# Rewriting the skipped general path as loops, and moving the bound check, the flag load and the low-part products in an attention-and-gated-MLP kernel

## The chip, the cores and the metric

The kernel runs on one core of a Trainium2 chip. The metric is the device time of one execution in microseconds (us). A core has a tensor engine (PE, whose weight loads are listed as PEld), a vector engine (DVE), a scalar engine (ACT), GpSimd (POOL) and SyncE (SP), each with its own queue of instructions that it works through in order; they wait for each other by semaphores. Here SP issues nearly all DMAs, and ACT issues output DMAs too.

## The reference

First a recurrent linear attention over 768 positions for 4 batches and 8 heads of 48, then a gated MLP on the result.

```python
for t in range(S):                       # S = 768, state is D x D per head, D = 48
    cur = einsum('bhd,bhe->bhde', u * k_t, v_t)
    y[:, :, t] = einsum('bhd,bhde->bhe', r_t, state + cur)
    state = w_t[..., None] * state + einsum('bhd,bhe->bhde', k_t, v_t)
x = y as (3072 tokens, 384)
out = (sigmoid(x @ w_gate) * (x @ w_val)) @ w_out      # 384 -> 1536 -> 384
```

## The kernel before

The 768 positions are cut into 6 blocks of 128; a block with its 4 batches is 512 tokens, and the attention of one batch in one block is a unit `q` of 24. The MLP runs over the 6 blocks `n` and, inside each, over 12 pieces `f` of the hidden width. All its products are made from a high and a low part of each operand: `whi` and `wlo` of the weights, `x` in two parts, and of the hidden values `hh` (high) and `hl` (low); each product is three (low x high, high x low, high x high).

One step (n, f) of the MLP in the later blocks: `gate` makes nine products into the bank `pg`, `sigmoid` (ACT) reads it into `sg`; `value` makes nine products into `pu`; `hidden` (DVE) multiplies into `sg`; `hidden_hi` (ACT, line 516) casts to `hh`; `hidden_lo` (DVE, line 520) subtracts to `hl`; `down_turned` makes nine products into the three banks `po` (line 546). A step's down products are issued one step later, after the value products of the next step; the variable `last` holds them back. At f = 11 `down_turned` also copies the three banks out (ACT for k = 0 and 2, line 554; in the last block DVE for k = 1, line 552) and issues the output DMAs (line 556).

Blocks 0 and 1 and the first attention units are ordered by a planner (`Plan`), which the change does not touch. From block 2 on the order is the loop at the end of `tile_kernel`: `n` over blocks 2 to 5, `j` over four batches, `i` over three pieces, so f = 3j + i. Between the MLP's parts stand those of the attention for block n + 1; in block 5 there are none left.

The fast path holds only while certain sums stay within bounds. After step (5, 0) `check_bounds` compares four tables of sums (lines 559 to 562, into `fine`), DVE adds them up into `count` (line 564), one product with a column of `ones` adds over the partitions into `total` (line 566), and DVE writes the word `flag` (line 567). At the very end every engine loads `flag` into a register (line 694) and branches: if it is not 0, `general` computes everything again in another way. With the inputs of the reference the flag is 0, and every engine jumps over `general`. Line 723 is the end of the program, where SP waits for the others and all engines meet in a barrier.

In the built program the weights of all 12 pieces, `flag`, `ones` and the states lie one behind the other in a pool of constants; `count` lies in another pool.

Of the kernel before, what the change touches and what calls it, by code (L numbers as in the profile page):

```python
# [9 lines left out]
F32 = mybir.dt.float32  # L10
# [11 lines left out]
P = 128  # L22
# [19 lines left out]


@with_exitstack
def general(ctx: ExitStack, tc: tile.TileContext, dec, tok, wts, u, out, whi, wlo, ident):


    nc = tc.nc
    pool = ctx.enter_context(tc.tile_pool(name="general", bufs=1))
    bank = ctx.enter_context(tc.tile_pool(name="banks", bufs=1, space=PSUM))  # L50
    rows = ctx.enter_context(tc.tile_pool(name="rows", bufs=1, space=bass.MemoryType.DRAM)).tile([NC_, B, C, DM], F32, name="rows")

    def tiles(name, shape, dtype=F32):
        return pool.tile(shape, dtype, name=name)

    raw, t, full, square = tiles("raw", [P, HW], mybir.dt.int64), tiles("t", [P, HW], I32), tiles("full", [P, HW]), tiles("square", [P, HW])
    for f in range(NFF):
        for half in range(2):
            cols = slice(half * HW, (half + 1) * HW)
            nc.sync.dma_start(raw, wts[f][:, cols])  # L60
# [12 lines left out]
            nc.vector.tensor_tensor(out=full, in0=full, in1=part, op=ALU.add)  # L73
            nc.scalar.copy(whi[f][:, cols], full)
            nc.vector.tensor_tensor(out=wlo[f][:, cols], in0=full, in1=whi[f][:, cols].bitcast(F32), op=ALU.subtract)
# [12 lines left out]
    ub = ul.unsqueeze(1).unsqueeze(3).broadcast_to(shape)  # L88
    py = [bank.tile([P, 512], F32, name=f"py{i}") for i in range(2)]
    values = tok.rearrange("(b c) t (n p o e) -> c n o t b p e", b=B, n=3, o=2, e=D)  # L90
    for c in range(NC_):
        for b in range(B):
            nc.sync.dma_start(d[:, b], dec[b * NC_ + c])
        with tc.For_i(0, C) as i:
            def at(first, step):
                return d[:, :, first:first + NP * step].rearrange("a b (p c) -> a b p c", c=step)[:, :, :, bass.ds(i, 1)].broadcast_to(shape)
            for o in range(2):
                for b in range(B):
                    nc.sync.dma_start(vb[64 * o:64 * o + D, b], values[c, 2, o, bass.ds(i, 1), b].partition_broadcast(D))
            nc.vector.tensor_tensor(out=kv, in0=vb, in1=at(WW, C), op=ALU.mult)  # L100
            nc.vector.tensor_tensor(out=mix, in0=kv, in1=ub, op=ALU.mult)
            nc.vector.tensor_tensor(out=mix, in0=mix, in1=state, op=ALU.add)
            nc.vector.tensor_tensor(out=mix, in0=mix, in1=at(WW + NP * C, C), op=ALU.mult)
            nc.vector.tensor_tensor(out=state, in0=state, in1=at(1, W1), op=ALU.mult)
            nc.vector.tensor_tensor(out=state, in0=state, in1=kv, op=ALU.add)
            for j in range(2):
                nc.tensor.matmul(py[j][:2, :DM], lhsT=heads, rhs=mix[:, 2 * j:2 * j + 2], start=True, stop=True)
                nc.scalar.copy(y[:, 2 * j:2 * j + 2], py[j][:2, :DM].rearrange("a (b p e) -> a b p e", b=2, e=D))
            for b in range(B):
                for o in range(2):  # L110
                    nc.sync.dma_start(
                        rows[c, b, bass.ds(i, 1)].rearrange("t (p o e) -> o t p e", o=2, e=D)[o], y[o:o + 1, b])
# [5 lines left out]
    def feed(n, b, turned):  # L118
        nc.sync.dma_start(x, rows[n, b])
        for k in range(NKT):  # L120
            nc.tensor.transpose(out=px[:, k * C:(k + 1) * C], in_=x[:, k * P:(k + 1) * P], identity=ident)
        px3 = px[:, :DM].rearrange("a (k c) -> a k c", c=C)
        nc.scalar.copy(xhi, px3)
        nc.vector.tensor_tensor(out=xlo, in0=px3, in1=xhi.bitcast(F32), op=ALU.subtract)
        for f in range(NFF):
            for s, acc in enumerate((pg, pu)):
                for k in range(NKT):
                    cols = slice(s * DM + k * P, s * DM + (k + 1) * P)
                    for j, (w, a) in enumerate(((wlo, xhi), (whi, xlo), (whi, xhi))):
                        nc.tensor.matmul(acc[:, :C], lhsT=w[f][:, cols], rhs=a[:, k], start=k == 0 and j == 0, stop=k == NKT - 1 and j == 2)  # L130
            nc.scalar.activation(gate, pg[:, :C], AF.Sigmoid)
            nc.vector.tensor_tensor(out=h, in0=pu[:, :C], in1=gate, op=ALU.mult)
            nc.scalar.copy(hh, h)
            nc.vector.tensor_tensor(out=hl, in0=h, in1=hh.bitcast(F32), op=ALU.subtract)
            for k in range(NKT if turned else 1):
                cols = slice(2 * DM + k * P, 2 * DM + (k + 1) * P)
                for j, (a, w) in enumerate(((hl, whi), (hh, wlo), (hh, whi))):
                    first, done = f == 0 and j == 0 and k == 0, f == NFF - 1 and j == 2
                    if turned:
                        nc.tensor.matmul(po[:, k * C:(k + 1) * C], lhsT=w[f][:, cols], rhs=a, start=first, stop=done, skip_group_check=True)  # L140
                    else:
                        nc.tensor.matmul(po[:, :DM], lhsT=a, rhs=w[f][:, 2 * DM:], start=first, stop=done)
        nc.scalar.copy(x, po[:, :DM])
        if turned:
            to = out[n].rearrange("(k p b c) -> b p k c", p=P, b=B, c=C)[b]
            nc.sync.dma_start(to, x.rearrange("p (k c) -> p k c", c=C))
        else:
            nc.sync.dma_start(out[n].rearrange("(b c e) -> b c e", b=B, c=C)[b], x)

    for n in range(NC_):  # L150
        for b in range(B):
            feed(n, b, n >= 2)


class Plan:
# [49 lines left out]
def tile_kernel(ctx: ExitStack, tc: tile.TileContext, dec: bass.AP, tok: bass.AP, wts: bass.AP, u: bass.AP, out: bass.AP):  # L205
# [41 lines left out]
    nc.gpsimd.memset(fine, 1.0)  # L247
    flag = const.tile([1, 1], I32, name="flag")
    ones = const.tile([P, 1], F32, name="ones")
    nc.gpsimd.memset(ones, 1.0)  # L250
    state = [const.tile([L, NP, D], F32, name=f"state{b}") for b in range(B)]

# [285 lines left out]
    def down_turned(n, f, i0, i1):  # L538

        hh, hl = hid["hi", n, f, i0], hid["lo", n, f, i0]  # L540
        for k in range(NKT):
            if f == 0:
                po[n, k] = ps1.tile([P, 512], F32, tag=f"po{k}", name=f"po{n}_{k}")
            cols = slice(2 * DM + k * P, 2 * DM + (k + 1) * P)
            for j, (h, w) in enumerate(((hl, whi), (hh, wlo), (hh, whi))):
                nc.tensor.matmul(po[n, k], lhsT=w[f][:, cols], rhs=h, start=f == 0 and j == 0, stop=f == NFF - 1 and j == 2)  # L546
            if f == NFF - 1:
                o = p1.tile([P, B * C], F32, tag=f"ot{k}", name=f"o{n}_{k}")
# [9 lines left out]
    def check_bounds():  # L558
# [1 line left out]
        nc.vector.tensor_scalar(out=fine[:, 1], in0=acc_x, scalar1=0.0, scalar2=0.0, op0=ALU.mult, op1=ALU.is_equal)  # L560
        nc.vector.tensor_scalar(out=fine[:, 2, :NFF], in0=acc_s, scalar1=1e10, scalar2=None, op0=ALU.is_le)
        nc.vector.tensor_scalar(out=fine[:, 3, :NFF], in0=acc_t, scalar1=0.0, scalar2=None, op0=ALU.is_equal)
        count = p1.tile([P, 1], F32, name="count")
        nc.vector.tensor_reduce(out=count, in_=fine, op=ALU.add, axis=AX.XY)
        total = att_bank("total")
        nc.tensor.matmul(total[:1, :1], lhsT=ones, rhs=count, start=True, stop=True)
        nc.vector.tensor_scalar(out=flag, in0=total[:1, :1], scalar1=float(P * 4 * NG), scalar2=None, op0=ALU.not_equal)
# [104 lines left out]
    for n in range(2, NC_):  # L672
        for j in range(B):
            trio = steps((n + 1) * B + j) if n + 1 < NC_ else nothing
            for i in range(3):
# [13 lines left out]
                last.append(a)  # L689
                if n == NC_ - 1 and j == 0 and i == 0:  # L690
                    check_bounds()
    down_turned(*last.pop())
    own.close()
    with tc.If(nc.values_load(flag[:1, :1]) != 0):
        general(tc, dec, tok, wts, u, out, whi, wlo, ident)


# [31 lines left out]
```

## Time and profile before

| | us |
|---|---|
| median of 3 runs | 598.0 |
| the 3 runs | 598.21, 598.0, 595.76 |
| span of the profiled execution, first to last instruction | 593.7 |
| the profiled execution's own time | not given beyond its span |
| PE busy in the span | 555.1 (93%) |
| DVE busy | 332.6 (56%) |
| ACT busy | 200.2 (34%) |
| POOL busy | 96.4 (16%) |

The span is the time from the first to the last instruction of the core; the time of a run contains what lies around it too. Busy time counts computing instructions; loads of registers, branches and waits are not in it, but are listed by source line with their durations. In rows of groups, "x9" is the number of instructions, the first number of a timeline row is the start, the second the time to the end of the last of them. PEclk, the clock granted to PE, is 9 to 10 tenths in all slices but a few at the start, where it is 7 or 8; the mean is 0.989.

### The profile page before, as it was taken

How to read it: one execution, taken by the hardware profiler on the slowest of the kernel's cores; microseconds unless marked ns; L12 is line 12 of the kernel's file. 1: busy time of each engine (PE TensorE's matmuls, PEld its weight loads, DVE VectorE, ACT ScalarE, POOL GpSimd, SP SyncE). 2: the span in 40 equal slices, each digit the busy share in tenths (PEclk: the TensorE clock that was granted, in tenths of full speed). 3: DMA queues.
4: the chain of work that ended last, by engine and by line, in shares of the span. 5: the costliest groups of instructions: out<-in, count | busy, mean ns of one | idle time of the engine just before them, and what ended most of it. 6: DMA issues, size and time to landing. Idle time of an engine off the chain costs nothing.

```text
span 593.7 us, 14287 instructions
## 1 busy us (share of the span) xinstructions
PE 555.1 (93%) x6330; PEld 478.6 (81%) x6330; DVE 332.6 (56%) x571; ACT 200.2 (34%) x397; POOL 96.4 (16%) x86
## 2 busy tenths in 40 slices
PE   4477799999999999999999999999999999999995
PEld 3366699999999999888888888888888888788884
DVE  4989889989675762254644644644544554212121
ACT  2648783434333322322212322212322212222221
POOL 3342011102220503002202202202202200000000
PEclk9998799999999999999999999999999999999999
DMA  8887930022243221122032042032032000100001
GB/s 238 269 332 285 363 94 2 1 88 71 73 135 97 82 70 60 54 87 73 18 88 78 17 135 87 3 87 83 24 124 86 3 1 2 40 15 0 1 0 60
DMA packets 11479, 50.84 MB, mean 86 GB/s; under 512 B 1312, under 2 KB 2464, under 8 KB 9872
## 3 DMA queue, kind: packets, MB, share of 16 engines
q1 hardware_dynamic: 8672, 45.38, 23.7%
q10 hardware_dynamic: 2736, 4.46, 2.0%
q8 instruction: 52, 0.85, 0.6%
q14 instruction: 19, 0.16, 0.1%
HBM read 45.11 MB, written 4.72 MB: 84 GB/s over the span
## 4 chain that ended last, share of the span: by engine, by line
PE 86%; DVE 7%; DMA 3%; issue 1%; ACT 1%; SPq 0%; ACTq 0%; DVEq 0%
PE pu L494 25%; PE pg L494 25%; PE po L546 16%; PE po L529 8%; PE pa L461 3%; PE pa L390 2%; PE pa L400 2%; DMA wraw<-wts 2%; PE pk L373 1%; PE px L473 1%; PE pv L437 1%; DVE eg L341 1%; DMA pin<-dec 1%; PE pa L437 1%; DVE full L275 1%
## 5 line engine op out<-in xcount | busy, mean ns | idle before, releaser
L494 PE MATMUL pu<-x,w 128*128 128x256 f32 (+1 forms) x864 | 171.4, 343 | 0.0
L494 PE MATMUL pg<-x,w 128*128 128x256 f32 (+1 forms) x864 | 169.0, 341 | 1.2 <-DVE w L287 1.2
L494 PEld LDWEIGHTS pg<-x,w 128*128 128x128 f32 x864 | 137.9, 192 | 19.4 <-DVE w L287 1.6
L494 PEld LDWEIGHTS pu<-x,w 128*128 128x128 f32 x864 | 136.7, 192 | 17.1
L512 DVE TENSOR_TENSOR sg<-pu,sg 128x256 f32<-128x256 f32 (+1 forms) x96 | 53.4, 556 | 145.0 <-PE pu L494 144.0
L516 ACT CAST hh<-sg 128x256 fp32r<-128x256 f32 (+1 forms) x96 | 49.1, 512 | 171.2 <-DVE sg L512 170.8
L505 ACT ACTIVATE sg<-pg 128x256 f32<-128x256 f32 (+1 forms) x96 | 46.9, 489 | 139.0 <-PE pg L494 137.7
L546 PE MATMUL po<-hh,w 128*128 128x512 f32 x288 | 89.1, 390 | 0.0
L334 POOL TENSOR_TENSOR bon<-tok,a 128x384 f32<-128x384 f32 x24 | 34.9, 1456 | 277.3 <-DVE a L330 277.3
L520 DVE TENSOR_TENSOR hl<-sg,hh 128x256 fp32r<-128x256 f32 (+1 forms) x96 | 55.2, 575 | 39.1 <-ACT hh L516 39.0
L546 PEld LDWEIGHTS po<-hh,w 128*128 128x128 f32 x288 | 54.1, 188 | 10.8
L546 PE MATMUL po<-hl,w 128*128 128x512 f32 x144 | 58.7, 407 | 0.2 <-DVE hl L520 0.2
L323 POOL TENSOR_TENSOR bon<-tok,ub 128x384 f32<-128x384 f32 x24 | 32.3, 1345 | 114.1 <-DMA tok<-tok 38.4
L529 PE MATMUL po<-w,hh 128*128 128x384 f32 x192 | 49.7, 340 | 0.0
L468 DVE TENSOR_TENSOR bon<-pa,bon 128x192 f32<-128x192 f32 x48 | 15.6, 352 | 48.0 <-PE pa L461 47.9
L529 PE MATMUL po<-w,hl 128*128 128x384 f32 x96 | 34.5, 359 | 6.0 <-DVE hl L520 6.0
L368 ACT ACTIVATE junk<-eg 112x1032 bf16<-112x1032 f32 x24 | 25.6, 1066 | 29.7 <-DVE eg L358 29.6
L529 PEld LDWEIGHTS po<-w,hh 128*128 128x128 f32 x192 | 35.5, 192 | 0.0
L341 DVE TENSOR_TENSOR_SCAN eg<-pin,ends 112x516 f32<-112x516 f32 x24 | 30.0, 1249 | 5.0 <-DMA pin<-dec 5.0
L546 PEld LDWEIGHTS po<-hl,w 128*128 128x128 f32 x144 | 27.0, 188 | 6.2 <-DVE hl L520 0.6
L358 DVE TENSOR_TENSOR_SCAN eg<-pin,heads 112x516 f32<-112x516 f32 x24 | 29.7, 1237 | 0.0
L326 POOL TENSOR_TENSOR bon<-bon,tok 128x384 f32<-128x384 f32 x24 | 27.4, 1140 | 1.7
(68 smaller groups left out, 502.4 us busy)
## 6 DMA issues: line engine op xcount, KB each, us to landing
pin<-dec SPq DMA_DIRECT2D x23, 675.5 KB, 5.3
tok<-tok SPq DMA_DIRECT2D x24, 576.0 KB, 5.8
wraw<-wts SPq DMA_DIRECT2D x12, 1152.0 KB, 12.3
y<-o ACTq DMA_DIRECT2D x11, 256.0 KB, 2.1
y<-o ACTq DMA_DIRECT2D x8, 192.0 KB, 1.9
pin<-dec SPq DMA_DIRECT2D x1, 448.0 KB, 4.0
y<-o SPq DMA_DIRECT2D x1, 256.0 KB, 2.9
pin<-dec SPq DMA_DIRECT2D x1, 227.5 KB, 2.8
```

The costliest lines, as they stand in the source:

```text
L323: nc.gpsimd.tensor_tensor(out=bon[q], in0=tk[q][:, 0:DM], in1=ub, op=ALU.mult)
L326: nc.gpsimd.tensor_tensor(out=bon[q], in0=bon[q], in1=tk[q][:, DM:2 * DM], op=ALU.mult)
L334: nc.gpsimd.tensor_tensor(out=by_head(bon[q]), in0=by_head(tk[q][:, 2 * DM:]), in1=a0, op=ALU.mult)
L341: nc.vector.tensor_tensor_scan(out=e[:, 516:0:-1], data0=t[:, 516:0:-1], data1=ends[:, 516:0:-1], initial=0.0, op0=ALU.mult, op1=ALU.add,)
L358: nc.vector.tensor_tensor_scan(out=e[:, WW:WW + 516], data0=t[:, 0:516], data1=heads[:, 0:516], initial=0.0, op0=ALU.mult, op1=ALU.add,)
L494: nc.tensor.matmul(t, lhsT=w[f][:, cols], rhs=x[n][:, a, k, i0 * C:i1 * C], start=k == 0 and j == 0, stop=k == NKT - 1 and j == 2)
L505: nc.scalar.activation(sg, hid["g", n, f, i0], AF.Sigmoid)
L512: nc.vector.tensor_tensor(out=sg, in0=hid["u", n, f, i0], in1=sg, op=ALU.mult)
L516: nc.scalar.copy(hh, hid["s", n, f, i0])
L520: nc.vector.tensor_tensor(out=hl, in0=hid["s", n, f, i0], in1=hid["hi", n, f, i0].bitcast(F32), op=ALU.subtract)
L529: nc.tensor.matmul(po[n, i][:, :DM], lhsT=h[:, c], rhs=w[f][:, 2 * DM:], start=f == 0 and j == 0, stop=f == NFF - 1 and j == 2,)
L546: nc.tensor.matmul(po[n, k], lhsT=w[f][:, cols], rhs=h, start=f == 0 and j == 0, stop=f == NFF - 1 and j == 2)
```

## The change

Five edits:

1. `general` is written as loops on the device instead of unrolled Python loops, keeps its weights in a scratch tensor in DRAM (`flat`) instead of in `whi` and `wlo`, and no longer takes these two as arguments. In the built program the part that is jumped over has these numbers of instructions:

| engine | before | after |
|---|---|---|
| PE | 7421 | 234 |
| DVE | 1344 | 234 |
| ACT | 1112 | 186 |
| SP | 626 | 327 |
| POOL | 133 | 176 |

2. `down_turned` makes the product with `hl` last instead of first, at f = 11 of blocks 2 to 5.
3. The sum over the partitions and the writing of `flag` are taken out of `check_bounds` into `add_bounds`, which is called after step (5, 3) instead of after (5, 0).
4. `flag` is loaded into the registers ahead of the last `down_turned` instead of behind it.
5. `count` becomes a constant tile of its own; this puts the states, the weights and some other tiles 32 bytes further on in the built program.

```diff
-def general(ctx: ExitStack, tc: tile.TileContext, dec, tok, wts, u, out, whi, wlo, ident):
+def general(ctx: ExitStack, tc: tile.TileContext, dec, tok, wts, u, out, ident):
...
-    for f in range(NFF):
+    with tc.For_i(0, NFF) as f:
...
-    for c in range(NC_):
+    with tc.For_i(0, NC_) as c:
...
-        for f in range(NFF):
+        with tc.For_i(0, NFF) as f:
+            nc.sync.dma_start(cur, flat[bass.ds(f, 1)].rearrange("o a c -> (o a) c"))
+            nc.scalar.copy(w2["hi"], cur)
+            nc.vector.tensor_tensor(out=w2["lo"], in0=cur, in1=w2["hi"].bitcast(F32), op=ALU.subtract)
...
-    for n in range(NC_):
-        for b in range(B):
-            feed(n, b, n >= 2)
+    with tc.For_i(0, 2 * B) as m:
...
+    with tc.For_i(0, NC_ - 2) as n:
+        with tc.For_i(0, B) as b:
...
@@ tile_kernel
+    count = const.tile([P, 1], F32, name="count")
@@ down_turned
-            for j, (h, w) in enumerate(((hl, whi), (hh, wlo), (hh, whi))):
+            three = [(hh, wlo), (hh, whi), (hl, whi)] if f == NFF - 1 else [(hl, whi), (hh, wlo), (hh, whi)]
+            for j, (h, w) in enumerate(three):
                 nc.tensor.matmul(po[n, k], lhsT=w[f][:, cols], rhs=h, start=f == 0 and j == 0, stop=f == NFF - 1 and j == 2)
@@ check_bounds
-        count = p1.tile([P, 1], F32, name="count")
         nc.vector.tensor_reduce(out=count, in_=fine, op=ALU.add, axis=AX.XY)
+
+    def add_bounds():
         total = att_bank("total")
         nc.tensor.matmul(total[:1, :1], lhsT=ones, rhs=count, start=True, stop=True)
         nc.vector.tensor_scalar(out=flag, in0=total[:1, :1], scalar1=float(P * 4 * NG), scalar2=None, op0=ALU.not_equal)
@@ the loop of blocks 2 to 5
                 if n == NC_ - 1 and j == 0 and i == 0:
                     check_bounds()
+                if n == NC_ - 1 and j == 1 and i == 0:
+                    add_bounds()
+    wrong = nc.values_load(flag[:1, :1])
     down_turned(*last.pop())
     own.close()
-    with tc.If(nc.values_load(flag[:1, :1]) != 0):
-        general(tc, dec, tok, wts, u, out, whi, wlo, ident)
+    with tc.If(wrong != 0):
+        general(tc, dec, tok, wts, u, out, ident)
```

How this moves instructions is seen in the order in which they stand on each engine. A name is that of a tile with its indices (`po5_0` is the bank for block 5, k = 0; `hl5_0_11` the low part of block 5, f = 11) and a running number. PE, around the bound sum, before: it stands behind the down products of step (4, 11).

```order
L546 MATMUL po4_2_5394<-hl4_0_11_6078,w11_1682 128x512
L546 MATMUL po4_2_5394<-hh4_0_11_6076,w11_1682 128x512 x2
L566 MATMUL total_6140<-count_6138,ones_97 1x1 [waits DVE_49,PE_49]
L494 MATMUL pg5_0_1_6143<-x5_5379,w1_373 128x512 [waits Activation_49]
L494 MATMUL pg5_0_1_6143<-x5_5379,w1_373 128x512 x8
```

PE, around the bound sum, after: it stands behind the down products of step (5, 2), and no longer waits for DVE.

```order
L561 MATMUL po5_2_6175<-hl5_0_2_6204,w2_557 128x512
L561 MATMUL po5_2_6175<-hh5_0_2_6202,w2_557 128x512 x2
L582 MATMUL total_6251<-count_98,ones_97 1x1 [waits PE_49]
L508 MATMUL pg5_0_4_6254<-x5_5380,w4_787 128x512 [waits Activation_49]
L508 MATMUL pg5_0_4_6254<-x5_5380,w4_787 128x512 x8
```

The sum has moved three steps on, and a gate group follows it as before. PE, end of the program, before:

```order
L546 MATMUL po5_2_6178<-hh5_0_10_6493,w10_1558 128x512 x2
L546 MATMUL po5_0_6170<-hl5_0_11_6531,w11_1682 128x512 [waits DVE_49]
L546 MATMUL po5_0_6170<-hh5_0_11_6529,w11_1682 128x512 [waits Activation_49]
L546 MATMUL po5_0_6170<-hh5_0_11_6529,w11_1682 128x512
L546 MATMUL po5_1_6174<-hl5_0_11_6531,w11_1682 128x512
L546 MATMUL po5_1_6174<-hh5_0_11_6529,w11_1682 128x512 x2
L546 MATMUL po5_2_6178<-hl5_0_11_6531,w11_1682 128x512
L546 MATMUL po5_2_6178<-hh5_0_11_6529,w11_1682 128x512 x2
L694 TENSOR_LOAD flag_96 [waits DVE_49]
L694 COMPARE_AND_BRANCH
```

PE, end of the program, after:

```order
L561 MATMUL po5_2_6175<-hh5_0_10_6493,w10_1559 128x512 x2
L710 TENSOR_LOAD flag_96 [waits DVE_49]
L561 MATMUL po5_0_6167<-hh5_0_11_6529,w11_1683 128x512 [waits Activation_49]
L561 MATMUL po5_0_6167<-hh5_0_11_6529,w11_1683 128x512
L561 MATMUL po5_0_6167<-hl5_0_11_6531,w11_1683 128x512 [waits DVE_49]
L561 MATMUL po5_1_6171<-hh5_0_11_6529,w11_1683 128x512 x2
L561 MATMUL po5_1_6171<-hl5_0_11_6531,w11_1683 128x512
L561 MATMUL po5_2_6175<-hh5_0_11_6529,w11_1683 128x512 x2
L561 MATMUL po5_2_6175<-hl5_0_11_6531,w11_1683 128x512
L713 COMPARE_AND_BRANCH
```

The first two of the last nine products now wait for `hh` (ACT), the third for `hl` (DVE), and the load stands ahead of all nine. SP, end of the program, before:

```order
L301 DMA pin23_5607<-dec 112x1544 [waits DMAHW3_49,DVE_49,PE_49]
L306 DMA tok23_5609<-tok 128x1152 [waits DMAHW4_49,PE_49,Pool_49]
L556 DMA y<-o5_1_6551 128x512 [waits DMAHW0_49,DVE_49]
L694 TENSOR_LOAD flag_96 [waits DVE_49]
L694 COMPARE_AND_BRANCH
```

SP, end of the program, after:

```order
L315 DMA pin23_5608<-dec 112x1544 [waits DMAHW3_49,DVE_49,PE_49]
L320 DMA tok23_5610<-tok 128x1152 [waits DMAHW4_49,PE_49,Pool_49]
L710 TENSOR_LOAD flag_96 [waits DVE_49]
L571 DMA y<-o5_1_6558 128x512 [waits DMAHW0_49,DVE_49]
L713 COMPARE_AND_BRANCH
```

The load changes places with SP's last output DMA. On ACT and DVE it likewise stands behind `hidden_hi` and `hidden_lo` of the last step and ahead of the copies of the last outputs.

More of the change, by code (lines that the diff above doesn't have):

```diff
@@ L50, in general @@
     bank = ctx.enter_context(tc.tile_pool(name="banks", bufs=1, space=PSUM))
-    rows = ctx.enter_context(tc.tile_pool(name="rows", bufs=1, space=bass.MemoryType.DRAM)).tile([NC_, B, C, DM], F32, name="rows")
+    far = ctx.enter_context(tc.tile_pool(name="far", bufs=1, space=bass.MemoryType.DRAM))
+    rows = far.tile([NC_, B, C, DM], F32, name="rows")
+    flat = far.tile([NFF, P, 3 * DM], F32, name="flat")
     def tiles(name, shape, dtype=F32):
@@ L56, in general @@
     raw, t, full, square = tiles("raw", [P, HW], mybir.dt.int64), tiles("t", [P, HW], I32), tiles("full", [P, HW]), tiles("square", [P, HW])
-    for f in range(NFF):
+    with tc.For_i(0, NFF) as f:
         for half in range(2):
             cols = slice(half * HW, (half + 1) * HW)
-            nc.sync.dma_start(raw, wts[f][:, cols])
+            nc.sync.dma_start(raw, wts[bass.ds(f, 1), :, cols].rearrange("o a c -> (o a) c"))
             words = raw.bitcast(I32).rearrange("a (c w) -> a c w", w=2)
@@ L73, in general @@
             nc.vector.tensor_tensor(out=full, in0=full, in1=part, op=ALU.add)
-            nc.scalar.copy(whi[f][:, cols], full)
-            nc.vector.tensor_tensor(out=wlo[f][:, cols], in0=full, in1=whi[f][:, cols].bitcast(F32), op=ALU.subtract)
+            nc.sync.dma_start(flat[bass.ds(f, 1), :, cols].rearrange("o a c -> (o a) c"), full)
     state, kv, mix = (tiles(n, [L, B, NP, D]) for n in ("state", "kv", "mix"))
@@ L90, in general @@
     values = tok.rearrange("(b c) t (n p o e) -> c n o t b p e", b=B, n=3, o=2, e=D)
-    for c in range(NC_):
+    decs = dec.rearrange("(b c) a w -> b c a w", b=B)
+    with tc.For_i(0, NC_) as c:
         for b in range(B):
-            nc.sync.dma_start(d[:, b], dec[b * NC_ + c])
+            nc.sync.dma_start(d[:, b], decs[b, bass.ds(c, 1)].rearrange("o a w -> (o a) w"))
         with tc.For_i(0, C) as i:
@@ L98, in general @@
                 for b in range(B):
-                    nc.sync.dma_start(vb[64 * o:64 * o + D, b], values[c, 2, o, bass.ds(i, 1), b].partition_broadcast(D))
+                    nc.sync.dma_start(vb[64 * o:64 * o + D, b], values[bass.ds(c, 1), 2, o, bass.ds(i, 1), b].rearrange("x t p e -> (x t) p e").partition_broadcast(D))
             nc.vector.tensor_tensor(out=kv, in0=vb, in1=at(WW, C), op=ALU.mult)
@@ L111, in general @@
                     nc.sync.dma_start(
-                        rows[c, b, bass.ds(i, 1)].rearrange("t (p o e) -> o t p e", o=2, e=D)[o], y[o:o + 1, b])
+                        rows[bass.ds(c, 1), b, bass.ds(i, 1)].rearrange("x t (p o e) -> o (x t) p e", o=2, e=D)[o], y[o:o + 1, b])
     x, px = tiles("x", [P, DM]), bank.tile([P, 512], F32, name="px")
@@ L117, in general, with feed @@
     pg, pu, po = (bank.tile([P, 512], F32, name=n) for n in ("pg", "pu", "po"))
-    def feed(n, b, turned):
-        nc.sync.dma_start(x, rows[n, b])
+    cur = tiles("cur", [P, 3 * DM])
+    w2 = {i: tiles("w" + i, [P, 3 * DM], F32R) for i in ("hi", "lo")}
+    zero = tiles("zero", [P, DM])
+    none = tiles("none", [P, DM], F32R)
+    nc.vector.memset(zero, 0.0)
+    nc.vector.tensor_copy(out=none, in_=zero)
+    def feed(source, turned):
+        nc.sync.dma_start(x, source)
         for k in range(NKT):
@@ L124, in feed @@
         nc.vector.tensor_tensor(out=xlo, in0=px3, in1=xhi.bitcast(F32), op=ALU.subtract)
-        for f in range(NFF):
+        nc.tensor.matmul(po[:, :DM], lhsT=none[:, :P], rhs=none, start=True, stop=False, skip_group_check=True)
+        with tc.For_i(0, NFF) as f:
+            nc.sync.dma_start(cur, flat[bass.ds(f, 1)].rearrange("o a c -> (o a) c"))
+            nc.scalar.copy(w2["hi"], cur)
+            nc.vector.tensor_tensor(out=w2["lo"], in0=cur, in1=w2["hi"].bitcast(F32), op=ALU.subtract)
             for s, acc in enumerate((pg, pu)):
@@ L128, in feed @@
                     cols = slice(s * DM + k * P, s * DM + (k + 1) * P)
-                    for j, (w, a) in enumerate(((wlo, xhi), (whi, xlo), (whi, xhi))):
-                        nc.tensor.matmul(acc[:, :C], lhsT=w[f][:, cols], rhs=a[:, k], start=k == 0 and j == 0, stop=k == NKT - 1 and j == 2)
+                    for j, (w, a) in enumerate((("lo", xhi), ("hi", xlo), ("hi", xhi))):
+                        nc.tensor.matmul(acc[:, :C], lhsT=w2[w][:, cols], rhs=a[:, k], start=k == 0 and j == 0, stop=k == NKT - 1 and j == 2)
             nc.scalar.activation(gate, pg[:, :C], AF.Sigmoid)
@@ L136, in feed @@
                 cols = slice(2 * DM + k * P, 2 * DM + (k + 1) * P)
-                for j, (a, w) in enumerate(((hl, whi), (hh, wlo), (hh, whi))):
-                    first, done = f == 0 and j == 0 and k == 0, f == NFF - 1 and j == 2
+                for j, (a, w) in enumerate(((hl, "hi"), (hh, "lo"), (hh, "hi"))):
                     if turned:
-                        nc.tensor.matmul(po[:, k * C:(k + 1) * C], lhsT=w[f][:, cols], rhs=a, start=first, stop=done, skip_group_check=True)
+                        nc.tensor.matmul(po[:, k * C:(k + 1) * C], lhsT=w2[w][:, cols], rhs=a, start=False, stop=False, skip_group_check=True)
                     else:
-                        nc.tensor.matmul(po[:, :DM], lhsT=a, rhs=w[f][:, 2 * DM:], start=first, stop=done)
+                        nc.tensor.matmul(po[:, :DM], lhsT=a, rhs=w2[w][:, 2 * DM:], start=False, stop=False, skip_group_check=True)
+        nc.tensor.matmul(po[:, :DM], lhsT=none[:, :P], rhs=none, start=False, stop=True, skip_group_check=True)
         nc.scalar.copy(x, po[:, :DM])
-        if turned:
-            to = out[n].rearrange("(k p b c) -> b p k c", p=P, b=B, c=C)[b]
-            nc.sync.dma_start(to, x.rearrange("p (k c) -> p k c", c=C))
-        else:
-            nc.sync.dma_start(out[n].rearrange("(b c e) -> b c e", b=B, c=C)[b], x)
-    for n in range(NC_):
-        for b in range(B):
-            feed(n, b, n >= 2)
+    with tc.For_i(0, 2 * B) as m:
+        feed(rows.rearrange("n b c e -> (n b) c e")[bass.ds(m, 1)].rearrange("o c e -> (o c) e"), False)
+        nc.sync.dma_start(out.rearrange("n (b c e) -> (n b) c e", b=B, c=C)[bass.ds(m, 1)].rearrange("o c e -> (o c) e"), x)
+    with tc.For_i(0, NC_ - 2) as n:
+        with tc.For_i(0, B) as b:
+            feed(rows[bass.ds(n + 2, 1), bass.ds(b, 1)].rearrange("o i c e -> (o i c) e"), True)
+            to = out.rearrange("n (k p b c) -> n b p k c", p=P, b=B, c=C)[bass.ds(n + 2, 1), bass.ds(b, 1)].rearrange("o i p k c -> (o i p) k c")
+            nc.sync.dma_start(to, x.rearrange("p (k c) -> p k c", c=C))
 class Plan:
```

## The prediction

> **What bounds the kernel now.** I read the span first, then the busy time by stretch, then the chain that ended last.
>
> ```profile
> span 593.7 us, 14287 instructions
> PE 86%; DVE 7%; DMA 3%; issue 1%; ACT 1%; SPq 0%; ACTq 0%; DVEq 0%
> 300.00:505.00 205.00, 205.00 (x2214) 166.68 (x2201) 103.46 (x181) 55.08 (x108) 34.69 (x25) 1.00 0.19 59
> 574.85 2.04 PE pu L494 x9
> 580.97 2.05 PE pu L494 x9
> 585.24 2.35 PE po L546 x9
> ```
>
> TensorE (PE) is the bound: from 300 to 505 us it is busy 205.00 of 205 us at a granted clock of 1.00 (third row, first two numbers after the colon, clock near the end). In the last blocks a step is nine gate, nine value and nine down products; two value groups stand 580.97 - 574.85 = 6.12 us apart, nine products take 2.04 us, one 0.227. No edit touches the number of those products, so all that can be gained is in places where PE waits, and behind its last product. The first such place is the sum of the bounds, in block 5. The timeline there (start, duration, engine; the idle time before in brackets):
>
> ```profile
> 512.16 2.20 PE L494 MATMUL pu<-x,w 128*128 128x512 f32 x9
> 515.78 0.61 PE L546 MATMUL po<-hh,w 128*128 128x512 f32 x2
> 516.46 0.17 DVE L559 TENSOR_SCALAR fine<-acc_d 112x24 f32<-112x24 f32 x1
> 516.89 0.25 DVE L564 TENSOR_REDUCE count<-fine 128x1 f32<-128x96 f32 x1
> 517.26 0.11 PEld L566 LDWEIGHTS total<-count,ones 128*1 128x1 f32 x2 [1.28 <-PE po L546]
> 517.29 0.19 PE L566 MATMUL total<-count,ones 128*1 128x1 f32 x2 [0.89 <-DVE count L564]
> 519.60 2.21 PE L494 MATMUL pu<-x,w 128*128 128x512 f32 x9
> ```
>
> From value group to value group it is 519.60 - 512.16 = 7.44 us, 1.32 over a step: PE stands until VectorE (DVE), which starts the five check operations only at 516.46, has written `count`. The second place is the end:
>
> ```profile
> 583.84 0.62 ACT L516 CAST hh<-sg 128x512 fp32r<-128x512 f32 x1 [2.18 <-DVE sg L512]
> 584.43 0.61 PE L546 MATMUL po<-hh,w 128*128 128x512 f32 x2
> 584.49 0.69 DVE L520 TENSOR_TENSOR hl<-sg,hh 128x512 fp32r<-128x512 f32 x1 [0.69 <-ACT hh L516]
> 585.58 0.62 PE L546 MATMUL po<-hh,w 128*128 128x512 f32 x2
> 586.24 0.59 ACT L554 COPY o<-po 128x512 f32<-128x512 f32 x1 [1.78 <-PE po L546]
> 586.93 0.69 DVE L552 COPY o<-po 128x512 f32<-128x512 f32 x1 [1.75 <-PE po L546]
> 587.61 0.59 ACT L554 COPY o<-po 128x512 f32<-128x512 f32 x1 [0.78 <-PE po L546]
> 587.65 0.34 SPq L556 DMA_DIRECT2D y<-o  x1
> 588.23 0.36 ACTq L556 DMA_DIRECT2D y<-o  x1
> L694 POOLq COMPARE_BRANCH  x1: 45/45/45, 518.3 to 518.3; - x1
> L694 PEldq TENSOR_LOAD <-flag x1: 488/488/488, 585.3 to 585.3; - x1
> L694 PEldq COMPARE_BRANCH  x1: 3697/3697/3697, 585.9 to 585.9; - x1
> L694 DVEq TENSOR_LOAD <-flag x1: 536/536/536, 586.9 to 586.9; - x1
> L694 SPq TENSOR_LOAD <-flag x1: 480/480/480, 588.0 to 588.0; - x1
> L694 SPq COMPARE_BRANCH  x1: 45/45/45, 588.6 to 588.6; - x1
> L694 SPq EVENT_SEMAPHORE  x8: 17/17/17, 591.7 to 592.3; - x8
> L694 ACTq TENSOR_LOAD <-flag x1: 597/597/597, 588.6 to 588.6; - x1
> L694 ACTq COMPARE_BRANCH  x1: 54/54/54, 589.3 to 589.3; - x1
> L694 ACTq EVENT_SEMAPHORE  x1: 17/17/17, 592.4 to 592.4; - x1
> L723 SPq EVENT_SEMAPHORE  x10: 17/28/28, 592.4 to 593.6; - x10
> L723 POOLq DRAIN  x3: 34/82/106, 518.7 to 593.4; - x3
> ```
>
> The first nine rows are the timeline, the rest the lines 694 (load and branch) and 723 (end) with the start of the first and last instruction of each kind. After its last DMA issue (587.65 + 0.34 = 587.99) the queue of SyncE (SP) loads the flag (480 ns), branches at 588.6, and its next instruction starts only at 591.7: 3.1 us lie behind a branch of 45 ns. Then come its eight waits (to 592.3), eight more at line 723, and the closing barrier to 593.7. ScalarE (ACT) shows the same: branch 589.3, next 592.4. GpSimd (POOL) does not: branch 518.3, next 518.7.
>
> **The change, part by part.** The sum is made against the span of 593.7. The time of that execution itself is not given; the median of the three runs, 598.0, lies 4.3 us above the span (their range 595.76 to 598.21 makes it 2.1 to 4.5), and I leave that remainder as it is.
>
> *Bound sum three steps later.* DVE makes `count` where it did; the product with `ones` now stands behind the down products of step 2, when `count` is some 18 us old. So PE's stall goes. What the product itself costs stays: its first weights load starts at 517.26, and the value group at 519.60 puts the gate group before it at 519.60 - 2.04 = 517.56, so 0.30 us. Gain 1.32 - 0.30 = 1.02; between 0 (PE stalls there for another reason) and 1.32 (the product hides in the stream). I take 1.02, since both rows are of this very product. What is queued behind: the flag operation on DVE waits for the product, ahead of step 4's `sg`; that needs value products over 4 us later (two groups of 2.04), so it waits for nothing new. ACT's copies of block 4's outputs and POOL's early flag load (POOL has nothing left to do) are not on the path.
>
> *Low-part products last, in the last f of blocks 2 to 5.* In blocks 2 to 4 these come one step later than their `hl`, without a wait in the stretch that is 205 of 205 busy: 0, covered by the gate and value groups between; without that cover it would be the end's wait again, 0.47. At the end it counts: PE's two products before start at 584.43, so the next could start at 584.43 + 2 x 0.227 = 584.88. They start at 585.58 - 0.227 = 585.35, because the first needs `hl` (DVE, to 584.49 + 0.69 = 585.18). Now the first two need `hh` only (ACT, to 584.46) and the third, at 585.34, needs `hl`, just there. Gain 0.47; at least 0 (`hl` as late as before for a product that comes first), at most the 0.47.
>
> *Flag load ahead of the last down products.* Five loads move. SP: the load can run as soon as the flag is written, tens of us before its last DMA; that DMA was behind nothing, and gets behind a load long done. So the load leaves SP's tail, and the branch takes its place at 588.0 instead of 588.6: gain 0.6 (bounds 0.48, the load alone, and 0.6); I take the rows' difference, which has the steps around the load in it. ACT: 0.6 leaves its tail too, its load moves behind the `hh` cast, where ACT idles 1.78 us until its copy; DVE's 536 ns moves behind `hl`, 1.75 us idle before its copy: 0 on both, and if the cover were gone their copies would be late by up to 0.6. PE: the load (488 ns) now stands ahead of the last nine products. It was started at 585.3, when the nine products ahead of it were only beginning, so PE's queue runs at least nine products (2 us) ahead of the array. The nine products of the step before cover it: 0 taken; without the cover the load starts at 584.66 with the last of them, PE goes on at 584.66 + 0.59 = 585.25, and 0.37 of the 0.47 is lost.
>
> *General path as loops.* It is not executed (flag 0: all branch). What is jumped over shrinks, counted in the built program, from 133 to 176 instructions on POOL, 1112 to 186 on ACT, 1344 to 234 on DVE, 626 to 327 on SP. In the traced run POOL's 133 cost 0.4 us from branch to next instruction, SP's 626 3.1. SP decides the end. Is 327 near or far?
>
> ```profile
> q8 instruction: 52, 0.85, 0.6%
> q14 instruction: 19, 0.16, 0.1%
> y<-o ACTq DMA_DIRECT2D x11, 256.0 KB, 2.1
> y<-o SPq DMA_DIRECT2D x1, 256.0 KB, 2.9
> L546 PEld LDWEIGHTS po<-hh,w 128*128 128x128 f32 x288 | 54.1, 188 | 10.8
> ```
>
> 1.01 MB of instruction packets for 14287 instructions are at most 71 bytes each, so 327 instructions are about 21 KB; the small packets (0.16 MB / 19) have 8.4 KB. POOL's jump is about one small packet, SP's new one more than two. I take it as far, at the old 3.1 us: gain 0. The other bound is POOL's 0.4; then SP would meet the landing of the last outputs: its DMA starts 0.47 earlier, at 587.18, and lands 2.9 later, at 590.08; ACT's starts at 587.76 and lands 2.1 later, at 589.86. Against SP's 588.0 - 0.47 + 3.1 = 590.6 that is 0.5 to 0.6 more (all before the 1.02 is taken off, which shifts everything). [...]
>
> Sum: 1.02 + 0.47 + 0.6 = 2.1 us. SP stays last: ACT's branch would come at 588.23 + 0.36 - 0.47 = 588.12, its next instruction 3.1 later at 591.2, while SP reaches its wait for ACT at about 591.7 (sixteen waits from 590.6, 1.1 us). Span 593.7 - 2.1 = 591.6, time **595.9**, 0.35% faster. About 0.5%, 3.0 us, is what a measurement of this kernel can tell from no change.
>
> **Rivals.**
> 1. SP's jump is near: 2.1 + 0.6 = 2.7, time 595.3. For it: POOL's 0.4 us. Against: 21 KB against packets of 8.4.
> 2. PE's load isn't covered: 2.1 - 0.37 = 1.7, 596.3. For it: nothing in the trace shows the load between two groups. Against: its start at 585.3.
> 3. The bound sum keeps its stall: 0.47 + 0.6 = 1.1, 596.9. For it: the weights' idle of 1.28 is put down to PE's own po, not to DVE. Against: the matrix row names `count`.
> 4. Slower: `count` moves among the constants and shifts all weights by 32 bytes in the built program, off a multiple of 64. If LDWEIGHTS (188 ns, below the 227 of a product) grew beyond 227, each of the 27 x 48 = 1296 products of blocks 2 to 5 would pay the excess: 1.6 ns pays back the 2.1, 4 ns (a load of 231) gives 598.0 + 5.2 - 2.1 = 601.1. Nothing in the trace speaks for it; no tile lies so.
>
> **How the numbers follow.** Forecast 0.64, rival 1 0.14, rival 2 0.10, rival 3 0.08, rival 4 0.04. The range goes from 593.7 (the lowest run, 595.76, less 2.1; it takes in 595.3) to 597.5 (the lower bounds of all terms, which leave the 0.48 of SP's load alone), and leaves out rival 4 and the tails. Faster by over 0.5%: no case reaches 3.0 us by itself, rival 1 lacks 0.3 and the forecast 0.9, and the runs spread over 2.5: a third of rival 1 and a sixth of the forecast make 0.15. Slower: rival 4, 0.04. Same: 0.81.
>
> **What would show it.** Right, if in the changed profile the value groups around the check stand 6.12 us apart and about 6.4 around the sum; if the last nine products follow without a gap; if the loads stand before the last outputs' DMA; and if SP's branch is followed by 3.1 us of nothing. Rival 1 shows as 0.4 us there, rival 2 as a gap in front of the last nine, rival 3 as a step of over 7 us, rival 4 as LDWEIGHTS over 220 ns. It is wrong if the end is set by the outputs' landing, or if the time around the span changes.

## The result: 0.68% slower, and the profile after

| | before | after |
|---|---|---|
| median of 6 runs, us | 596.95 (595.76 to 598.21) | 601.14 (600.22 to 602.38) |
| span of the profiled execution, us | 593.7 | 598.5 |
| time of that execution, us | | 600.22 |

The ratio is 1.0068 (95% interval 1.0053 to 1.0084). The forecast was 595.9 us, with a range from 593.7 to 597.5, so it missed by 5.2 us and in sign. Wherever a run has both numbers, its time is 1.7 to 1.8 us above its span (600.22 and 598.5 here); of the 4.3 us that the prediction left as a remainder the other 2.6 came from its base, 598.0, the median of executions slower than the profiled one. The first rows of the page after, and the row of 300 to 505 us (after the span's two numbers: busy us and instructions of PE, PEld, DVE, ACT, POOL, then the granted clock):

```profile
span 598.5 us, 14287 instructions
PE 560.1 (94%) x6330; PEld 478.2 (80%) x6330; DVE 333.0 (56%) x571; ACT 200.4 (33%) x397; POOL 96.2 (16%) x86
...
300.00:505.00 205.00, 205.00 (x2270) 164.40 (x2270) 101.67 (x178) 54.58 (x106) 34.68 (x25) 1.00 0.19 59
```

The number of instructions on PE is the same, the clock is the same 1.00, and PE was and is busy in all of the 205 us. But PE is busy 560.1 us instead of 555.1. So no wait was added: the same products take longer. The chain that ended last, after, says which:

```profile
249.47 2.11 PE pu L508 x9
...
580.33 2.10 PE pu L508 x9
...
586.63 2.10 PE pu L508 x9
588.73 4.21 PE po L561 x18
592.94 0.02 issue
```

Nine products take 2.10 us instead of 2.04 (one 0.233 instead of 0.227; this time from one product's start to the next is called the pitch below), and two value groups stand 586.63 - 580.33 = 6.30 us apart instead of 6.12. The groups by form (busy us, then mean ns of one), before and after, with the weights load of the after kernel:

```profile
L494 PE MATMUL pg<-x,w 128*128 128x512 f32 x432 | 106.1, 390 | 0.0
L494 PE MATMUL pg<-x,w 128*128 128x256 f32 x432 | 62.9, 292 | 1.2 <-DVE w L287 1.2
```

```profile
L508 PE MATMUL pg<-x,w 128*128 128x512 f32 x432 | 108.8, 396 | 0.0
L508 PE MATMUL pg<-x,w 128*128 128x256 f32 x432 | 63.3, 293 | 1.3 <-DVE w L301 1.3
...
L561 PEld LDWEIGHTS po<-hh,w 128*128 128x128 f32 x288 | 54.0, 188 | 11.9
```

Only the products of 512 columns (blocks 2 to 5) have become longer, from 390 to 396 ns; those of 256 columns in the blocks before have not, and a weights load of the down products takes 188 ns as before. (The mean of one is longer than the pitch, because neighbouring products overlap: in the timeline before, the nine gate products of 572.64 last 2.20 us, and the value products behind them start after 2.04, at 574.68.)

**The balance.** The first value group of block 2 in the chain stands at 248.90 before:

```profile
248.90 2.10 PE pu L494 x9
```

From there to the last value group it is 580.97 - 248.90 = 332.07 us before and 586.63 - 249.47 = 337.16 after: +5.09. Within this the bound sum gained 1.00 (next section but one), so the slower products cost 6.09 us over 47 steps of 27, 4.8 ns each. From the last value group to the end it is 12.73 before and 598.5 - 586.63 = 11.87 after: -0.86. The start of block 2 is 0.57 later, which is scatter: in the profiles of this study that group starts between 246.2 and 253.1 us, whatever the kernel. 5.09 - 0.86 + 0.57 = 4.80, the difference of the spans.

### The profile page after: what moved, and what is told of

The parts are those of the page before. It is cut to its first block, busy times and chain, and to the rows that moved or that the text cites. A ratio compares the mean times of both kernels' runs of the same rounds, so it can differ in the third digit from the quotient of the medians.

```text
span 598.5 us, 14287 instructions
## 1 busy us (share of the span) xinstructions
PE 560.1 (94%) x6330; PEld 478.2 (80%) x6330; DVE 333.0 (56%) x571; ACT 200.4 (33%) x397; POOL 96.2 (16%) x86
## 4 chain that ended last, share of the span: by engine, by line
PE 88%; DVE 7%; issue 1%; DMA 1%; ACT 1%; POOL 0%; ACTq 0%; SPq 0%; DVEq 0%; POOLq 0%
PE pu L508 25%; PE pg L508 25%; PE po L561 17%; PE po L543 8%; PE pa L475 3%; PE pa L404 2%; PE pa L414 2%; PE pk L387 1%; PE px L487 1%; DMA ub<-u 1%; PE pv L451 1%; DVE eg L372 1%; PE pa L451 1%; DVE full L289 1%; DVE eg L355 1%
## 5 line engine op out<-in xcount | busy, mean ns | idle before, releaser
L508 PE MATMUL pg<-x,w 128*128 128x256 f32 (+1 forms) x864 | 172.1, 345 | 1.3 <-DVE w L301 1.3
L561 PE MATMUL po<-hh,w 128*128 128x512 f32 x288 | 90.5, 396 | 0.0
L387 PE MATMUL pk<-ident,pin 112*128 112x112 f32 x96 | 14.7, 279 | 14.7 <-DVE pin L361 9.8
```

The source lines that it names most:

```text
L508: nc.tensor.matmul(t, lhsT=w[f][:, cols], rhs=x[n][:, a, k, i0 * C:i1 * C], start=k == 0 and j == 0, stop=k == NKT - 1 and j == 2)
```

## The experiments

Diffs are against the kernel before where nothing else is said. Times are medians, each beside runs of the kernel before on the same chip.

### Which edit slows the products

**Edit 5 alone**: `count` as a constant, everything else as before.

```diff
+    count = const.tile([P, 1], F32, name="count")
...
-        count = p1.tile([P, 1], F32, name="count")
```

> The kernel before with edit 5 alone: count becomes a constant tile, so all weights lie 32 bytes further on (off a multiple of 64), the moving operands x, hh and hl stay. Theory A (the weights' address sets the pitch of the 512-column products): pitch 233 ns instead of 227 in blocks 2 to 5, about 6 us slower than before (ratio 1.010), bound-sum stall of 1.3 us still there. Rival B (one of the moved instructions or the loops slows the products): pitch 227, no change from before. Rival C (the distance between weights and moving operands counts, modulo 64): as A, 6 us slower.

603.33 us against 597.26, ratio 1.0096 (1.0068 to 1.0124). Its chain in block 5:

```profile
546.30 2.10 PE pu L495 x9
548.40 2.10 PE po L547 x9
```

So this edit alone brings the 2.10 us. **All edits but this one**: the after kernel with `count` back in its old pool.

```diff
-    count = const.tile([P, 1], F32, name="count")
...
+        bank["count"] = count = p1.tile([P, 1], F32, name="count")
```

> The changed kernel with count put back into its old pool, so that nothing is shifted; the other four edits stay. Theory A and rival C: pitch 227 ns, and the forecast's gains are seen alone, about 2.1 us faster than before (ratio 0.9965; step around the bound sum 0.3 us long, last nine products without a gap, loads ahead of the last output). Rival B: pitch 233 ns and about 4 us slower than before, as the changed kernel.

596.11 against 597.26, ratio 0.998 (0.9958 to 1.0002), nine products in 2.04 us again:

```profile
584.23 2.04 PE pu L507 x9
```

These two settle the edit. In the built program its whole effect on these products is that the weights begin 32 bytes further on (26848 instead of 26816 for the first tile) and that x, `hh` and `hl` stay where they were: the pool of constants grows by 32 bytes, and the pool that `count` left, which lies between, shrinks by 32.

### Is it the place of the weights, or their distance from the moving operands?

**Both 32 bytes on**: `count` as a constant, and a spare column of 32 bytes ahead of the pool that holds x, `hh` and `hl`.

```diff
+    count = const.tile([P, 1], F32, name="count")
+    lower = p1.tile([P, 1], F32, name="lower")
+    nc.gpsimd.memset(lower, 1.0)
...
-        count = p1.tile([P, 1], F32, name="count")
```

> The kernel before with weights and the moving operands x, hh, hl all 32 bytes further on (a spare tile of 4 bytes more per partition, whose slot is 32, beside count). Theory A: pitch 233 ns, about 6 us slower. Rival C (only the distance modulo 64 counts): pitch 227 ns, no change. Rival B: no change.

**Weights 64 bytes on, moving operands 32**:

```diff
+    count = const.tile([P, 1], F32, name="count")
+    spare = const.tile([P, 1], F32, name="spare")
+    nc.gpsimd.memset(spare, 1.0)
...
-        count = p1.tile([P, 1], F32, name="count")
```

> The kernel before with weights 64 bytes further on (a multiple of 64 again) and the moving operands 32 further on. Theory A: pitch 227 ns, no change. Rival C: pitch 233 ns, about 6 us slower. A third one, D (any operand off a multiple of 64 slows): slower here too, and more so with both shifted.

The first gave 597.33 against 597.26, ratio 1.0003 (0.9985 to 1.0022), the second 604.23, ratio 1.0122 (1.0097 to 1.0148). Their chains in block 5, the first and then the second:

```profile
546.60 2.04 PE pu L497 x9
548.64 2.04 PE po L549 x9
```

```profile
547.47 2.10 PE po L549 x9
549.57 2.10 PE pg L497 x9
```

Weights off a multiple of 64 cost nothing here if the moving operands are off by as much (2.04 us for nine products); with weights on a multiple of 64 the products are slow if the moving operands are not (2.10). What counts is the distance of the two. Rival 4, which put it on the alignment of the weights, falls as worded.

### Which distances are good

Moving operands alone further on, by 64, 128, 192 and 256 bytes; the weights stay. The first was timed, of the others there is a profile each.

```diff
+    lower = p1.tile([P, 16], F32, name="lower")     # 32, 48, 64 in the others
+    nc.gpsimd.memset(lower, 1.0)
```

> The kernel before with only the moving operands (and the tiles around them) 64 bytes further on, so that distance grows by 64. Theory C with modulus 64: pitch 227 ns, no change. C with modulus 128: pitch 233 ns, 6 us slower (ratio 1.010).

> The kernel before with x, hh and hl 128 bytes further on and the weights where they were, so the distance between the two operands of each product is 128 bytes off a multiple of 256. If distances of 128 bytes repeat: nine products in 2.04 us, a step of 6.12 us. If it takes 256 bytes to repeat: over 2.05 us, a step of 6.15 us or more, since 64 bytes gave 2.06 us. If only the distance within 64 bytes counts, and the 2.06 us at 64 bytes had another cause: 2.04 us.

> The same with 192 bytes. If distances repeat at 128 bytes: as 64 bytes, 2.06 us for nine products, a step of 6.18 us. If they repeat at 256 bytes: anything above 2.04 us, and alike to 64 bytes only if the sign of the distance does not matter.

> The same with 256 bytes. If the distance repeats at 128 or at 256 bytes: 2.04 us for nine products, a step of 6.12 us. If any move of the tiles costs, whatever its size: 2.06 us or more.

Chains in block 5, in the order 64, 128, 192, 256:

```profile
546.41 2.06 PE po L548 x9
```

```profile
549.07 2.09 PE pg L496 x9
551.15 2.10 PE pu L496 x9
```

```profile
544.96 2.10 PE pg L496 x9
547.06 2.10 PE pu L496 x9
```

```profile
545.99 2.04 PE pu L496 x9
```

The second number that bears on this is the stretch from the start of block 2's first value group to the start of block 5's last one. In the traces of the five kernels that have all these distances at 0 and the bound sum in its old place it is 332.0 to 332.1 us, so a difference of 1 us shows in a single profile:

| moving operand minus weights, modulo 256 bytes | nine products, us | stretch, us more than before | kernels |
|---|---|---|---|
| 0 | 2.04 | -0.1; 0.0 | both on by 32; moving on by 256 |
| 32 | 2.10 | | only the hidden values on by 32 (below), its down products |
| 64 | 2.06 | 1.4 | moving on by 64 (ratio 0.9996, 0.9973 to 1.0018) |
| 128 | 2.09 to 2.10 | 5.1 | moving on by 128 |
| 192 | 2.10 | 6.4 | moving on by 192 |
| 224 | 2.10 | 6.0; 6.0 | edit 5 alone; weights on by 64, moving by 32 |
| 224 | 2.10 | 5.1, with 1.0 gained at the bound sum | after |

At 64 bytes the products came out between the two values expected; the 1.4 us that they cost are too small for the timing to show for certain. The single executions of 128, 192 and 256 took 603.70, 599.58 and 597.51 us beside 600.30 for one of the kernel before; a single time tells no difference here, since the start of block 2 alone scatters by 7 us.

A repeat at 64 or at 128 bytes is excluded by 2.10 at 192 against 2.06 at 64; a repeat at 256 fits all these rows. Larger repeats were not tried.

### Single operands

To see whether high and low weights count apart, weights were moved inside their tiles, which had to be made 64 bytes larger for that: both halves on by 16 bytes, and only the low half by 32.

```diff
-        raws[f] = const.tile([P, 3 * DM], I64, tag=f"w{f}", name=f"wraw{f}")
+        raws[f] = const.tile([P, 3 * DM + 8], I64, tag=f"w{f}", name=f"wraw{f}")[:, :3 * DM]
...
-        w = const.tile([P, 2, 3 * DM], F32R, tag=f"w{f}", name=f"w{f}")
-        whi[f], wlo[f] = w[:, 0], w[:, 1]
+        w = const.tile([P, 6 * DM + 16], F32R, tag=f"w{f}", name=f"w{f}")
+        whi[f], wlo[f] = w[:, 4:4 + 3 * DM], w[:, 3 * DM + 4:6 * DM + 4]     # both on by 16
+        whi[f], wlo[f] = w[:, 0:3 * DM], w[:, 3 * DM + 8:6 * DM + 8]         # or: low on by 32
```

> The kernel before with the high and low weights 16 bytes further on inside their tiles (12 tiles, each 64 bytes larger), nothing else off a multiple of 64. C as 'any distance that is no multiple of 64 is slow': pitch about 233 ns, 6 us slower. C as 'only which 32-byte half counts': pitch 227 ns, no change, since 16 bytes stay in the same half at the start.

> The kernel before with only the low weights 32 bytes further on inside their tiles; they serve one product of three. C: a third of the products get the slow pitch, mean 229 ns, 2 us slower (ratio 1.0035), and the timeline shows which interval pays: the one before the product with the low weights (while they are loaded) or the one behind its start. Rival A (the address of the weights tile as a whole) would give all or nothing: 227 or 233 throughout.

They gave 601.09 (ratio 1.0069, 1.0038 to 1.0101) and 602.95 (1.0085, 1.0053 to 1.0118) against 597.51. The second shows

```profile
546.65 2.08 PE po L546 x9
548.73 2.09 PE pg L494 x9
```

where a third of the products was to be slow. Neither answers the question, as the control shows, which has the larger tiles and no offset:

> The kernel before with weight tiles 64 bytes larger, as in the two kernels that shifted weights inside their tiles, but without any offset: a control for those two, since every second tile now lies an odd multiple of 64 bytes from the moving operands. If the 64 matters as little as with the moving operands 64 bytes on (228.6 ns there), pitch 227 to 229 ns and at most 2 us slower (ratio up to 1.003); then the offsets of 16 and 32 bytes made the 232 ns. If the larger tiles themselves cost it: pitch 232 ns, 5 us slower.

601.01 against 597.64, ratio 1.0046 (1.0023 to 1.0068), above the 1.003 of the first case expected. Tiles of 9280 bytes instead of 9216 (36 times 256) put every piece f 64 bytes off the one before, so the distances run through 0, 192, 128 and 64. Its value groups for the pieces 5 to 8, which lie 192, 128, 64 and 0 apart:

```profile
549.88 2.10 PE pu L494 x9
556.15 2.09 PE pu L494 x9
562.40 2.06 PE pu L494 x9
568.62 2.04 PE pu L494 x9
```

One execution gives all four paces of the table again. From value group to value group its steps in block 5 are 6.20, 6.27, 6.25 and 6.22 us and then repeat, with a mean of 6.235. Three groups each of 2.04, 2.06, 2.095 and 2.10 make steps with a mean of 6.22. So the size of a tile, too, costs by the distance it makes.

**Only the hidden values 32 bytes on** (their pool, behind a spare column):

```diff
+    gap = own.enter_context(tc.tile_pool(name="gap", bufs=1)).tile([P, 1], F32, name="gap")
+    nc.gpsimd.memset(gap, 1.0)
```

> The kernel before with only the pool of sg, hh and hl 32 bytes further on: the nine down products of a step have a moving operand off by 32 from the weights, the eighteen gate and value products of x have not. Theory C, by groups of products: down groups at 233 ns, the others at 227; a step of block 5 of 6.18 us, about 2.5 us slower (ratio 1.004). Rival E (one misplaced operand slows all products of the stream, as the low weights alone did): 6.30 us, 6 us slower.

601.38 against 597.64, ratio 1.0051 (1.0029 to 1.0072).

```profile
547.22 2.10 PE po L548 x9
549.32 2.08 PE pg L496 x9
551.40 2.04 PE pu L496 x9
553.44 2.10 PE po L548 x9
```

The down products, whose moving operand is off by 32, are slow, the value products are not, and the gate group between them, whose operands are 0 apart, takes 2.08. So the slow pitch is not lost at once: by 2.08 between 2.10 and 2.04, some six of the nine gate products still have it, an estimate from these three times. So the step is 6.22 us, between the 6.18 of theory C and the 6.30 of rival E.

### The terms of the sum by themselves

**The loops alone** (the after kernel without edits 2 to 5) and **the end alone** (edits 2 and 4 in the kernel before):

```diff
+            three = [(hh, wlo), (hh, whi), (hl, whi)] if f == NFF - 1 else [(hl, whi), (hh, wlo), (hh, whi)]
+            for j, (h, w) in enumerate(three):
...
+    wrong = nc.values_load(flag[:1, :1])
     down_turned(*last.pop())
...
+    with tc.If(wrong != 0):
```

> The kernel before with the general path as loops and nothing else (nothing is shifted). By the prediction: SP's jump over 327 instructions stays far, 3.1 us behind its branch, no change. Rival 1 of the prediction: SP's jump near, 0.5 us faster or a little more.

> The kernel before with low-part products last and the flag load ahead of the last down products, nothing else. By the prediction: 0.47 + 0.6 = 1.1 us faster (ratio 0.998); no gap ahead of the last nine products, step around the bound sum 7.44 us as before. Rival 2 of the prediction: a gap of up to 0.4 us ahead of the last nine, 0.7 us faster.

The loops alone: 597.12 against 597.64, ratio 1.0 (0.9981 to 1.0018), with SP's branch as far as before:

```profile
L707 SPq EVENT_SEMAPHORE  x8: 17/17/17, 593.3 to 593.9; - x8
...
L707 SPq COMPARE_BRANCH  x1: 45/45/45, 590.2 to 590.2; - x1
```

The end alone: 596.34, ratio 0.9977 (0.9958 to 0.9996). Its span is 594.1, its chain at the end

```profile
582.58 2.04 PE pu L494 x9
584.62 4.13 PE po L547 x18
588.75 0.02 issue
```

From the last value group to the last product it is 6.17 us; before, 585.24 + 2.35 - 580.97 = 6.62. That is 0.45 for the order of the products. From the last product to the end it is 594.1 - 588.75 = 5.35 against 593.7 - 587.59 = 6.11, 0.76 for the load.

### The change with the distance put right

The after kernel with two spare columns, which put weights and moving operands 64 bytes on from where they were before, 0 apart:

```diff
     count = const.tile([P, 1], F32, name="count")
+    spare = const.tile([P, 1], F32, name="spare")
+    nc.gpsimd.memset(spare, 1.0)
+    lower = p1.tile([P, 1], F32, name="lower")
+    nc.gpsimd.memset(lower, 1.0)
```

> The changed kernel with spare tiles, so that weights and moving operands x, hh, hl all lie 64 bytes further on than before: each at a multiple of 64, distance as before. Theory C (the distance of weights and moving operands modulo 64 counts): pitch 227 ns and all gains kept, about 2 us faster than before (ratio 0.9965). Rival S (any displacement of the weights by itself, 64 too): pitch 233 ns, about 4 us slower.

595.12 us against 597.51, ratio 0.9963 (0.9943 to 0.9984): faster than before and after. The version with `count` back in its old pool (0.998, 0.9958 to 1.0002) cannot be told from it.

```profile
531.45 2.04 PE pu L512 x9
533.49 2.04 PE po L565 x9
535.53 0.12 PE total L586 x2
535.65 2.28 PE pg L512 x9
537.93 2.04 PE pu L512 x9
```

## Why the prediction was wrong, point by point

**The step that failed is the one that is not in the sum: edit 5 at nothing.** The 27 x 48 = 1296 products were taken at 0.227 us because nothing changed their number and a weights load (188 ns) stays below it; so the prediction made its sum from the places where PE waits and from the end alone. The products have a price of their own for where their two operands lie, which no row of before could show, since there all these distances were 0 modulo 256. That 0.227 is not their only price, a row of before did show (248.90 above: 2.10 us for nine, behind attention products). The term is +6.1 us of slower products. Rival 4 had the 32 bytes and, at 4 ns per product, the time (601.1; measured 601.14), but gave it 0.04. That the time fits is luck: the 4 ns were an example, and they stood on a base 1 us above the median of the six runs. Its way was wrong too: its sign, LDWEIGHTS over 220 ns, is missing (188), and the alignment of the weights by itself costs nothing (both on by 32: ratio 1.0003). The words "no tile lies so" were the gap: that the trace holds no case of a new layout was read as evidence against it, where the range had to be opened.

**Bound sum, forecast 1.02.** The timeline after, around the sum:

```profile
535.75 2.26 PE L508 MATMUL pu<-x,w 128*128 128x512 f32 x9
...
540.05 0.09 PEld L582 LDWEIGHTS total<-count,ones 128*1 128x1 f32 x2 [0.37 <-issue]
...
542.37 2.26 PE L508 MATMUL pu<-x,w 128*128 128x512 f32 x9
```

6.62 us from value group to value group is 0.32 over the step of 6.30, where it was 1.32: gain 1.00. In the version with the distance put right it is 537.93 - 531.45 = 6.48, 0.36 over 6.12: gain 0.96. Right; rival 3 (a step of over 7 us) is out.

**Low-part products last, forecast 0.47.** The chain after has the last 18 products as one piece of 4.21 us behind the value group, with no gap. The end alone measured 0.45. There the weights load of the first product with `hl` still stands idle for 0.16 us until `hl` is there, but the product itself starts 0.23 us behind the one before it, without a gap. Right.

**Flag load ahead, forecast 0.6.** Lines 710 (load) and 713 (branch) after:

```profile
L710 SPq TENSOR_LOAD <-flag x1: 468/468/468, 540.4 to 540.4; - x1
L710 PEldq TENSOR_LOAD <-flag x1: 485/485/485, 586.5 to 586.5; - x1
```

```profile
L713 SPq EVENT_SEMAPHORE  x8: 17/17/17, 596.6 to 597.1; - x8
...
L713 PEldq COMPARE_BRANCH  x1: 353/353/353, 591.0 to 591.0; - x1
...
L713 SPq COMPARE_BRANCH  x1: 45/45/45, 593.4 to 593.4; - x1
...
L713 ACTq COMPARE_BRANCH  x1: 54/54/54, 593.9 to 593.9; - x1
L713 ACTq EVENT_SEMAPHORE  x1: 17/17/17, 597.1 to 597.1; - x1
```

SP loads at 540.4, far from the end, and branches behind its DMA; PE's load at 586.5 is covered by the value group (rival 2 is out). From the last product to the end it is 598.5 - 592.94 = 5.56 instead of 6.11: 0.55 here, 0.76 in the end alone; SP's jump itself takes from 2.9 us (the version put right) to 3.2 (after), which is a wider spread than the difference. The load's part without the jump is the time from the end of the last product to SP's branch: 1.02 us before, 0.45 both in the kernel after and in the end alone, a gain of 0.57. Right in kind and size.

**Loops, forecast 0.** From SP's branch to its next instruction it is 596.6 - 593.4 = 3.2 us: far, as assumed, and rival 1 (0.4) is out. ACT jumps over 186 instructions and also takes 3.2 (593.9 to 597.1). The number jumped over does not set the time alone: DVE, over 234, takes 1.5 us (592.3 to 593.8). What else sets it, no run shows. PE's branch did become near (353 ns instead of 3697 over 234 instructions instead of 7421), but PE's end does not set the end.

So the three gains together were 1.00 + 0.86 = 1.86 us in the after kernel (the slower pitch takes some 0.15 of the end's part: 0.06 in the value group, 0.09 in the 18 products, 4.21 against 4.12 in the version put right), forecast 2.1, and 6.1 us of slower products stood against them. With the median of six runs as base this is 596.95 - 1.86 + 6.09 = 601.18; measured were 601.14.

Blocks 2 to 4 lose less than block 5 (6.09 us over 47 steps are 0.13 per step, block 5 alone loses 0.18) because a part of their groups was slow already. There two thirds of the value and down groups stand behind attention products, and in the kernel before such a group takes 2.09 us or more, as in the first of these rows, and the others 2.04 to 2.05:

```profile
258.51 2.09 PE po L546 x9
262.65 2.04 PE pu L494 x9
```

The products of the 24 value groups behind attention start 242.6 ns apart on average before and 244.1 after; in the 12 behind other MLP products it is 226.6 and 233.3.

What stays open: why the distance counts; no run shows it. Nor is the distance the whole rule. With both weight halves on by 16 bytes, the value group of piece 2, 112 off modulo 256 in every block, takes 2.10 us in block 2 (263.68) and 2.05 in block 5 (530.01), where that of piece 6, as far off, takes 2.10 (555.07). Why the attention products leave a slow pitch behind them was not tried.

## What to carry to other kernels

Where products like these stand back to back, the offset of the weights' address against the moving operand's belongs in the cost of an edit (here nine took 2.04 us at 0 and 256 bytes, 2.06 to 2.10 at 32, 64, 128, 192 and 224): a new constant of 32 bytes per partition cost more here (6.1 us) than three real savings gained (1.9). Before a change that adds, drops or resizes a tile, compare the addresses in the built program, keep the distance with a spare column, and judge the change only then (ratio 0.9963 instead of 1.0068). When the only thing that an edit does to a busy stage is new to the trace, it has no price yet: widen the range instead of writing zero.

## What the runs showed of the hardware

- Products of 128x128 weights with 512 columns behind products of their own kind ran at 0.227 us each where the operands lay 0 modulo 256 bytes apart, at 0.229 for 64, and at 0.232 to 0.234 for 32, 128, 192 and 224, at a granted clock of 1.00; a weights load of the down products took 188 to 189 ns at 0, 64, 128, 192 and 224. Gate products of 256 columns showed no such difference at 0 and 224 (a mean of 292 and 293 ns).
- A slow pitch outlived its cause: 2.08 us for a group with distance 0 behind one that is 32 bytes off, then 2.04. Behind attention products, too, a down group with distance 0 took 2.09 us in the kernel before (258.51), the groups after it 2.04.
- In the after kernel a jump over 186 (ACT) or 327 (SP) instructions took 3.2 us to the next instruction, as SP's over 626 did before (3.1); DVE's over 234 took 1.5 and POOL's over 176 took 0.45.
